# Output rows stored run by run, and the first half's tiles leaving in the order third, first, second

## The chip, the cores and the metric

The kernel runs on one core of one Trainium2 chip. The metric is the time of one execution in microseconds (us), as the device measures it. Inside the core, TensorE (PE) multiplies, VectorE (DVE), ScalarE (ACT) and GpSimd (POOL) work elementwise, and SyncE (SP) issues most of the DMA transfers. The 16 DMA engines of the core move the data between its on-chip memory and the DRAM.

## The reference

A block-sparse attention is followed by a Fourier mixing layer with a two-layer network. For 4 batches, 8 heads, 768 positions and 64 columns per head, in float32:

```python
scores = scale * np.matmul(q, k.transpose(0, 1, 3, 2))
scores = np.where(mask, scores, -1000000000.0)        # mask: blocks of 32 positions
attn = np.exp(scores - scores.max(-1)); attn /= attn.sum(-1) + 1e-09
x = np.matmul(attn, v)          # (B, H, S, D) -> (B, S, H*D) = (4, 768, 512)
...
u = x + np.real(np.fft.fft(np.fft.fft(x, axis=1), axis=2))
un = (u - mean(u)) / np.sqrt(var(u) + 1e-06)
out = u + np.maximum(un @ w_ch1, 0.0) @ w_ch2         # 512 -> 2048 -> 512
```

## The kernel before

**Order of positions.** The 768 positions of a batch are held as six tiles of 128 partitions, not in their order in memory but as the Fourier step wants them. The table `_ORDER` (line 53) gives the runs of each tile: tile, first partition, number of runs, the jump from run to run, rows in a run, first row, step. Tiles 0 and 1 are two ascending runs of 64 rows with step 2 (rows 0, 2, ... and rows 1, 3, ...; then the same from row 128). Tiles 2, 3 and 4 are one single row, two descending runs of 63 rows (step -2), and one single row. Tile 5 is a single row, an ascending run of 63 and an ascending run of 64.

**The row lists.** `_rows` (line 80) turns this into transfers: for a tile it gives pairs of partitions and an access pattern in DRAM. Where the jump is positive, two runs go into one transfer whose outermost dimension is 2 (line 88). It has three uses: the output stores (line 1132), the loads of the sine and cosine tables (`table_s`, line 386), and a general path that runs only where the scores are too large for the fast path, which is not taken with these inputs.

**The halves.** Tiles 0, 1, 2 of a batch stand in a buffer `xA`, tiles 3, 4, 5 in `xB`. There are two of each, so a batch takes the buffer of the batch two before it. The attention writes its output into `xA` and `xB` (`place`, line 666: three transposes on PE, then one copy on ACT, line 675). The first such copy of batch 2 must wait until the stores of batch 0's `xA` have landed, and batch 3 for batch 1.

**The order of the work.** A Python planner writes the instruction order of every engine by hand; it keeps estimated times of the engines in `when`. The attention of batches is cut in slots (`slot`, line 1377). The mixing of an earlier batch is interleaved with it: its elementwise steps from the list `apart`, its large products from the list `late`. For `late`, batches 0, 1 and 2 have four rounds of two `quad` steps (first layer) and six `channels` steps (line 1118: 8 matmul instructions for one tile of the second layer, then one DVE addition into `x`, line 1125); in the last round `channels` calls `store` (line 1130), which issues the tile's transfers on SP. When the last tile of a half has been stored, the pair (batch, half) is added to `finished`. Before batch 2 or 3 places its first output into `xA`, the planner empties `late` until that pair is there (`until`, line 1432), and then gives the copy an estimated 9 us of delay (`LEAVES`), which changes its place among its neighbours and no wait.

**The last batch.** Its second layer is `outputs` (line 1171), which works on tile m of both halves at a time, in order 0, 1, 2 and in two rounds. Its last tile is stored in half-width pieces: the left half of `xA`'s tile on SP, the left half of `xB`'s tile on ACT's queue, then the right halves on SP (lines 1206 to 1233).

## Time and profile before

| What | us |
|---|---|
| Median of three timed runs (lowest to highest) | 1075.06 (1074.61 to 1076.39) |
| The profiled execution, by the same measure as the timed runs | 1075.65 |
| Its span, from the first to the last instruction | 1073.9 |
| PE busy in the span | 1033.3 (96%) |
| DVE, ACT, POOL busy | 669.5, 365.9, 240.5 |
| Written to DRAM | 6.29 MB |

Times in the views are microseconds from the start of the span. "SPq" and "ACTq" are the instruction queues of SP and ACT; a DMA row there is the time to issue a transfer, not to move it. The windows view gives for each stretch its length, the busy time of each engine with its count of instructions, then the TensorE clock that was granted (1.00 is full), the mean busy share of the core's 16 DMA engines, and GB/s. In the timeline, brackets hold the idle time just before a group of instructions and what ended it. The chain of waits is followed back from the last computing instruction.

### The profile page before, as it was taken

Reading aid. Unit: us, or ns where it says so; the run is one execution under the profiler, and the core shown is the slowest. Engines: PE = TensorE matmul, PEld = TensorE weight load, DVE = VectorE, ACT = ScalarE, POOL = GpSimd, SP = SyncE. Lnnn points to the kernel's source line nnn. Section 1 sums busy time; section 2 is a strip of 40 time slices with the busy share of each in tenths; the row PEclk is TensorE's granted clock in tenths of the full one; section 3 lists DMA queues with packets and bytes.
Section 4 is the critical chain, followed back from the end, with each engine's and each line's share of the span. In section 5 each row is a group of like instructions: output and inputs, shape, how many; then the busy total and the mean of one; then the engine's idle time right before and its main releaser. Section 6 shows DMA issues by size and latency. Waiting matters only on the chain.

```text
span 1073.9 us, 12481 instructions
## 1 busy us (share of the span) xinstructions
PE 1033.3 (96%) x4414; PEld 539.6 (50%) x4414; DVE 669.5 (62%) x1227; ACT 365.9 (34%) x736; POOL 240.5 (22%) x270
## 2 busy tenths in 40 slices
PE   8989999999999998999999998899999999999995
PEld 5333345445465453444435654354445554578584
DVE  6888795867746354755678363764456446774663
ACT  6978765564021022432441211434220121210210
POOL 1000173565000000554552001455420001000000
PEclk9999999999999999999999999999999999999998
DMA  7757422220000001231220001211000000000001
GB/s 209 224 170 223 107 46 45 45 45 15 1 1 1 0 3 52 52 55 28 41 54 0 1 1 35 69 29 25 8 14 1 1 0 36 25 1 1 0 15 47
DMA packets 120207, 46.26 MB, mean 43 GB/s; under 512 B 107836, under 2 KB 113226, under 8 KB 120138
## 3 DMA queue, kind: packets, MB, share of 16 engines
q1 hardware_dynamic: 118864, 44.66, 16.9%
q10 hardware_dynamic: 1242, 0.72, 0.3%
q8 instruction: 36, 0.59, 0.2%
q14 instruction: 33, 0.27, 0.1%
q0 software_dynamic: 32, 0.01, 0.0%
HBM read 36.72 MB, written 6.29 MB: 40 GB/s over the span
## 4 chain that ended last, share of the span: by engine, by line
PE 83%; DVE 5%; ACT 3%; DMA 3%; issue 2%; SPq 2%; POOL 0%; ACTq 0%; DVEq 0%
PE y L1122 22%; PE z L1066 15%; PE s L577 11%; PE o L651 9%; PE yp L1066 7%; PE yy L1185 6%; PE xp L1066 3%; PE zp L855 2%; DMA out_dram<-x 2%; PE s L587 1%; PE sp L718 1%; DVE t L1028 1%; SPq L690 1%; ACT e L597 1%; DMA wraw<-in_moe_w_ch_dram 1%
## 5 line engine op out<-in xcount | busy, mean ns | idle before, releaser
L637 POOL TENSOR_TENSOR acc<-acc,e 128x384 f32<-128x384 f32 x158 | 160.8, 1052 | 86.3 <-DVE e L607 67.4
L577 PE MATMUL s<-qT,kT 64*128 64x384 f32 x768 | 156.3, 523 | 16.8 <-DVE e L607 10.4
L651 PE MATMUL o<-e,vr 128*64 128x384 f32 x768 | 142.2, 498 | 2.2 <-DVE oT L659 2.2
L1125 DVE TENSOR_TENSOR x<-y,x 128x512 f32<-128x512 f32 x72 | 49.8, 691 | 131.5 <-PE y L1122 131.2
L1122 PE MATMUL y<-w_sb,hB 128*128 128x512 f32 x288 | 129.0, 599 | 0.3 <-DVE x L1125 0.3
L1122 PE MATMUL y<-w_sb,hA 128*128 128x512 f32 x288 | 128.2, 595 | 0.0
L607 DVE TENSOR_TENSOR e<-s,mask 128x768 f32<-128x768 f32 x88 | 80.1, 950 | 58.2 <-ACT s L605 49.2
L577 PEld LDWEIGHTS s<-qT,kT 64*128 64x128 f32 x768 | 64.7, 187 | 95.1 <-DVE e L607 24.4
L637 POOL TENSOR_TENSOR acc<-e 128x384 f32<-128x384 f32 x46 | 50.4, 1116 | 225.3 <-ACT e L597 127.3
L605 ACT ACTIVATE s<-s 128x768 f32<-128x768 f32 x88 | 66.9, 792 | 92.3 <-PE s L577 92.0
L597 ACT ACTIVATE e<-s 128x768 f32<-128x768 f32 x104 | 79.0, 809 | 48.6 <-PE s L587 35.8
L1066 PE MATMUL z<-unT,t 128*128 128x384 f32 x256 | 93.3, 487 | 0.5 <-DVE hA L1071 0.5
L1122 PEld LDWEIGHTS y<-w_sb,hB 128*128 128x128 f32 x288 | 54.0, 192 | 66.9 <-issue 66.1
L1122 PEld LDWEIGHTS y<-w_sb,hA 128*128 128x128 f32 x288 | 53.7, 190 | 62.5 <-issue 59.8
L651 PEld LDWEIGHTS o<-e,vr 128*64 128x64 f32 x768 | 47.9, 136 | 72.6 <-issue 67.7
L1071 DVE TENSOR_TENSOR hA<-z,hA 128x384 f32<-128x384 f32 x64 | 35.6, 557 | 70.8 <-PE z L1066 70.8
L1075 ACT ACTIVATE hA<-hA 128x384 f32<-128x384 f32 x64 | 33.5, 523 | 122.1 <-DVE hA L1071 122.0
L1066 PEld LDWEIGHTS z<-unT,t 128*128 128x128 f32 x256 | 48.4, 190 | 35.3 <-DVE hA L1071 2.5
L1075 ACT ACTIVATE hB<-hB 128x384 f32<-128x384 f32 x64 | 33.5, 523 | 86.4 <-DVE hB L1071 86.4
L938 POOL TENSOR_SCALAR st<-st 128x1 f32<-128x1 f32 x24 | 8.3, 346 | 207.1 <-DVE st L937 207.0
L1086 ACT COPY hA<-xp 128x384 f32<-128x384 f32 x32 | 15.3, 477 | 111.6 <-PE xp L1066 111.6
L1066 PE MATMUL xp<-unT,w_sb 128*128 128x384 f32 x128 | 47.4, 493 | 0.0
(207 smaller groups left out, 1432.5 us busy)
## 6 DMA issues: line engine op xcount, KB each, us to landing
wraw<-in_moe_w_ch_dram SPq DMA_DIRECT2D x32, 512.0 KB
vr<-in_v_dram SPq DMA_DIRECT2D x30, 192.0 KB
qb<-in_q_dram SPq DMA_DIRECT2D x44, 96.0 KB
kb<-in_k_dram SPq DMA_DIRECT2D x44, 96.0 KB
x<-oT SPq DMA_DIRECT2D x192, 12.0 KB
out_dram<-x SPq DMA_DIRECT2D x11, 252.0 KB
out_dram<-x SPq DMA_DIRECT2D x8, 256.0 KB
qr<-in_q_dram SPq DMA_DIRECT2D x24, 64.0 KB
```

Source lines behind the costliest of these rows:

```text
L577: nc.tensor.matmul(s[:, i, 0:HS], kT[rows, c * P:(c + 1) * P], qT[rows, queries], start=True, stop=u not in by_pe)
L597: nc.scalar.activation(out=e, in_=s[:, :, 0:HS], func=ACT.Exp, scale=scale)
L605: nc.scalar.activation(out=s[:, :, 0:HS], in_=s[:, :, 0:HS], func=ACT.Exp, scale=scale)
L607: nc.vector.tensor_tensor(out=e, in0=s[:, :, 0:HS], in1=m.broadcast_to([P, 2, HS]), op=ALU.mult)
L637: nc.gpsimd.tensor_add(out=acc[:, i, :], in0=start[:, i, :], in1=e[:, i, :])
L651: nc.tensor.matmul(o[D * i:D * i + D, :], vt[:, i, c, :], e[:, i, :], start=(c == 0), stop=(c == C - 1))
L1066: nc.tensor.matmul(to, a[:, k, :], c[:, k, :], start=(k == 0), stop=(k == ND // 2 - 1))
L1071: tt(out=to, in0=ps, in1=a, op=ALU.add)
L1075: nc.scalar.activation(out=h, in_=h, func=ACT.Relu)
L1122: nc.tensor.matmul(y, hs[0, half][:, l, m * P:(m + 1) * P], w2_sb[:, 4 * r + l, :], start=(l == 0), stop=(l == 3))
L1125: nc.vector.tensor_tensor(out=x[:, m, :], in0=y, in1=x[:, m, :], op=ALU.add)
L1185: nc.tensor.matmul(ps, a[:, k, :], c[k // 2][:, k % 2, :] if isinstance(c, list) else c[:, k, :], start=(k == 0), stop=(k == 3))
```

## The change

Two things change. In `_rows`, two runs go into one transfer only if the step is negative: the ascending pairs (tiles 0 and 1) become two transfers of 64 rows each, in the stores and in three of the four loads of the sequence tables; the descending pairs (tiles 2, 3, 4) stay as they are. And the first half's tiles are worked on in the order 2, 0, 1 in `channels` (all rounds); the second half's stay in the order 0, 1, 2. For the last batch, `outputs` takes the tiles in the order 2, 0, 1 for both halves, so the tile stored in pieces at the end is number 1 of each half.

```diff
-        if jump > 0:
+        if jump > 0 > step:
             got.append((p0, runs * n, bass.AP(tensor=at.tensor, offset=at.offset,
                                               ap=[[jump * row, runs], [step * row, n], col])))
             continue
...
-            if m == T - 1:
+            if m == out_of[half][-1]:
                 finished.add((b, half))
...
         last = b == B - 1
+        OUT = (2, 0, 1)
+        out_of = (OUT, OUT if last else (0, 1, 2))
...
-            if m == 0:
+            if m == OUT[0]:
                 output_left(m, 1)
                 output_left(m, 2)
...
-            if m == 0:
+            if m == OUT[0]:
                 output_left(m, 3)
                 output_left(m, 4)
...
-            rest += [(lambda r=r, m=m: outputs(r, m, m + 1 if m + 1 < T else None), 7 * 1.75)
-                     for m in range(T)]
+            rest += [(lambda r=r, m=m, after=after: outputs(r, m, after), 7 * 1.75)
+                     for m, after in zip(OUT, OUT[1:] + (None,))]
...
             rest += [(lambda r=r, half=half, m=m: channels(r, half, m), 3.45)
-                     for half in range(2) for m in range(T)]
+                     for half in range(2) for m in out_of[half]]
```

Compared as built, PE, DVE, ACT and POOL keep their numbers of instructions, and the kinds stand in the same order but for the tile numbers. SP's list has each `2x64x512` store replaced by two `64x512`, and each `128x1x385` table load by two `64x385`. At the end, ACT's queue has the transfers of 1, 2x63 and 1 rows where it had 1, 63 and 64.

## The prediction

> **What bounds the kernel now.** I read the page first, then the list of waits, then the chain of waits, and last the timeline and the windows around the two places to which these led. The page gives the shares of the chain by engine:

> ```profile
> PE 83%; DVE 5%; ACT 3%; DMA 3%; issue 2%; SPq 2%; POOL 0%; ACTq 0%; DVEq 0%
> ```

> PE is the path nearly everywhere, and the change leaves its instructions as they are. So only pauses of PE, and the end after the last product, can move the time. The list of waits (columns: us in total, times, longest) has two rows that belong together:

> ```profile
> ACT x L675 <- DMA out_dram<-x: 13.0, 2, 7.0
> PE s L577 <- DVE e L607: 10.4, 6, 4.4
> ```

> Twice, ACT waits for output stores before it may write into `xA`. The chain (start, us, what) shows both places and the prices of undisturbed work beside them:

> ```profile
> 399.09 3.44 PE y L1122 x8
> 408.18 9.62 DMA out_dram<-x
> 420.17 2.73 PE s L577 x8
> 422.90 4.13 PE y L1122 x8
> 442.42 1.49 PE s L577 x8
> 660.41 10.07 DMA out_dram<-x
> 672.80 2.77 PE s L577 x8
> 675.57 4.07 PE y L1122 x8
> ```

> The first gate in the timeline: SP issues the stores of batch 0's tiles 0, 1 and 2; then come ACT's, PE's and DVE's rows.

> ```profile
> 399.41 0.62 SPq L1133 DMA_DIRECT2D out_dram<-x  x1
> 403.28 0.56 SPq L1133 DMA_DIRECT2D out_dram<-x  x1
> 407.15 2.37 SPq L1133 DMA_DIRECT2D out_dram<-x  x3
> 411.36 0.58 ACT L992 COPY unT<-utp 128x512 f32<-128x512 f32 x1 [3.90 <-PE utp L991]
> 411.15 0.49 PE L674 MATMUL xt<-ident,oT 128*128 128x128 f32 x3
> 411.58 1.56 PE L577 MATMUL s<-qT,kT 64*128 64x384 f32 x8
> 413.07 2.80 PE L651 MATMUL o<-e,vr 128*64 128x384 f32 x16
> 417.95 0.48 ACT L675 COPY x<-xt 128x384 f32<-128x384 f32 x1 [6.00 <-DMA out_dram<-x]
> 419.16 1.82 DVE L607 TENSOR_TENSOR e<-s,mask 128x768 f32<-128x768 f32 x2 [6.49 <-ACT s L605]
> 420.17 2.73 PE L577 MATMUL s<-qT,kT 64*128 64x384 f32 x8 [4.30 <-DVE e L607]
> ```

> Read upward: PE stands 4.30 us for DVE's masking, DVE for ACT's exponential, and ACT's exponential is queued behind the copy L675, which waits 6.00 us for the stores. The copy's source was ready at 411.64 (411.15 + 0.49) and ACT free at 411.94. The second gate has the same shape:

> ```profile
> 662.96 0.58 ACT L992 COPY unT<-utp 128x512 f32<-128x512 f32 x1 [3.29 <-PE utp L991]
> 663.60 0.55 PE L674 MATMUL xt<-ident,oT 128*128 128x128 f32 x3 [0.68 <-ACT unT L992]
> 670.58 0.48 ACT L675 COPY x<-xt 128x384 f32<-128x384 f32 x1 [7.03 <-DMA out_dram<-x]
> 672.80 2.77 PE L577 MATMUL s<-qT,kT 64*128 64x384 f32 x8 [4.43 <-DVE e L607]
> ```

> Why the stores are so late is in the windows (length; busy time of each engine; then granted clock, busy share of the 16 DMA engines, GB/s):

> ```profile
> 400.50:401.00 0.50, 0.50 (x2) 0.19 (x1) 0.13 (x1) 0.00 (x0) 0.42 (x2) 1.00 0.10 25
> 402.00:408.00 6.00, 5.65 (x20) 2.84 (x19) 2.60 (x5) 1.17 (x2) 0.97 (x2) 1.00 0.13 45
> 408.00:412.00 4.00, 4.00 (x16) 2.08 (x16) 1.08 (x3) 0.58 (x1) 0.00 (x0) 1.00 0.13 51
> 420.00:422.00 2.00, 1.83 (x6) 0.94 (x8) 0.98 (x2) 1.38 (x4) 0.00 (x0) 0.61 0.23 67
> 422.00:424.00 2.00, 2.00 (x6) 0.66 (x3) 1.19 (x2) 1.25 (x2) 0.00 (x0) 0.54 0.50 85
> ```

> While only two-run stores are under way, the share is 0.13, which is 2 of 16 engines, and they move 51 GB/s, 25.5 GB/s each. The outermost dimension of these transfers is 2. One tile is 256 KB (262,144 bytes), or 5.1 us at that rate; three tiles in a row are 15.4 us, and from the first data at about 401 that gives 416.4, close to the 417.8 at which the chain sees them landed. The two-engine stores are the gate.

> **The change part by part.**

> *Gates.* Tile 2 goes first: its two-run transfer (252 KB) is issued at 399.4, has data from about 401 and ends near 406.3. Tile 0 follows at 403.3 and tile 1 at 407.15, each as two 64-row transfers. No window of before holds 64-row stores alone. At the end of the kernel 63- and 64-row pieces run beside a two-run one:

> ```profile
> 1061.50:1063.50 2.00, 0.52 (x3) 0.12 (x1) 0.42 (x1) 0.00 (x0) 0.00 (x0) 1.00 0.62 133
> ```

> 133 GB/s in that mixture is the slow bound: 2.0 us for a tile. The fast bound is 16 x 25.5 = 408 GB/s: 0.6 us. I take the slow one. The third store is issued from 407.15; for its two transfers I take 0.85 us (the issues above took 0.56 to 0.62 for one), to 408.0. Its data start some 1.3 us later (399.41 to the window in which data begin), and it is landed by 411.3 at the latest, by 409.9 by the fast bound. ACT is free at 411.94, so L675 no longer waits for DMA. Then ACT copies (0.48), its two exponentials take 1.51 (418.32 to 419.83 in before), and DVE's pair ends about 3.3 us after the copy began, as it does now (417.95 to 420.98): at about 415.3. PE's products L651 end at 415.87. Nothing holds the next scores. Even a landing 0.5 us later costs nothing, and each us after that costs one. At the second gate ACT is free at 663.54 and the source ready at 664.15 (663.60 + 0.55). The third store, tile 1's in the new order, begins to be issued there at 659.37, so by the same sum it lands by 663.5:

> ```profile
> 659.37 0.27 SPq L1133
> ```

> So both pauses go: 4.30 + 4.43 = 8.73 us. After each, the clock was granted at 0.61 and 0.54, and the first work was slow: scores 2.73 and 2.77 against 1.49, second-layer products 4.13 and 4.07 against 3.44. That is 1.24 + 1.28 + 0.69 + 0.63 = 3.84 us, which goes with the pauses. [...]

> What is late next? While PE paused, DVE (6.49 us) and ACT (6.00) were idle too, so no backlog is waiting on them. The loads of `kb`, queued on SP right behind the stores, are first used here, far later:

> ```profile
> 453.10 1.51 DVE L544 STREAM_TRANSPOSE kT<-kb 128x768 f32<-128x768 f32 x1
> ```

> They start earlier too, with the stores ahead of them shorter. The second half's stores stay in two-run form, and its copies showed no wait for DMA; both sides move together.

> *SP's extra issues.* Each tile 0 or 1 costs one issue more, some 0.3 to 0.6 us on SP. In the stretch above, SP had 3 us between tile stores. I take 0; without that cover it is 0.6 us per gate, still inside the margin of the copy.

> *Tables.* Three loads of 192 KB leave the two engines for many. The weight load behind the last of them is awaited once:

> ```profile
> 77.76 0.68 ACT L464 ACTIVATE wraw<-wraw 128x512 f32<-128x512 uint32 x1 [0.92 <-DMA wraw<-in_moe_w_ch_dram]
> ```

> PE runs on through that point on the chain, so between a gain of 0.9 and a loss of 0.6 (one more issue ahead of a weight load) I take 0.

> *Order of the tiles.* The additions into `x` and the second-layer products are the same in number and kind, for other tiles: 0. Batch 2's stores gate nothing: 0.

> *The end.* The last addition is over at 1062.48; what follows is stores.

> ```profile
> 1059.79 1.43 ACTq L1133 DMA_DIRECT2D out_dram<-x  x3
> 1062.06 0.42 DVE L1192 TENSOR_TENSOR x<-yy,x 128x256 f32<-128x256 f32 x1 [0.97 <-PE yy L1185]
> 1066.10 0.91 SPq L1133 DMA_DIRECT2D out_dram<-x  x2
> 1068.00:1071.00 3.00, 0.00 (x0) 0.00 (x0) 0.00 (x0) 0.00 (x0) 0.00 (x0) 0.50 0.15 45
> 1071.00:1071.50 0.50, 0.00 (x0) 0.00 (x0) 0.00 (x0) 0.00 (x0) 0.00 (x0) 0.50 0.00 0
> ```

> SP could not issue the last tile's pieces until 1066.10, 3.6 us after the addition: it was behind earlier two-run stores. The last piece (126 KB, again on two engines) then ran until about 1071. With the change the earlier stores of tiles 0 and 1 are spread, and the last piece on SP is two 64-row transfers, issued at 1062.5. But tile 4's halves are now two-run pieces of 126 KB, one on ACT's queue from 1059.8 and one on SP's from 1060.8. One such piece took about 3.7 us (1067.3 to 1071). If both use the same two engines, they take 7.4 us from about 1061.4, to 1068.8, and the 64-row pieces behind them end at about 1069.3: 1.7 us earlier than now. The bounds: if the two pieces don't share, the last data come at about 1066.5, 4.5 us earlier; if sharing costs each 5 us, 1071.9, 0.9 later. I take 1.7, since the two-run stores of before all show the same share of 2 engines and follow one another.

> *Sum.* 8.73 + 3.84 + 1.7 = 14.3 us. The profiled execution took 1075.65, so it becomes 1061.4. It was 0.59 above the median of 1075.06; the forecast for the median is 1060.8.

> **The rivals.**

> *The gain is swallowed later.* Some load that the pauses hid becomes the bound. Against it: after the gates the list of waits names one wait for a transfer,

> ```profile
> DVE oT L659 <- DMA x<-oT: 5.7, 1, 5.7
> ```

> and what that transfer moves is computed on the path itself, so it starts earlier too. Were all swallowed, only the end would gain: 1075.1 - 1.7 = 1073.4.

> *The gates open only in part*, because 64-row transfers spread over few engines. A tile on n engines takes 10.3/n us. On four that is 2.6, and tile 1 lands at 411.9; on three it lands at 412.7, which leaves 0.2 us at the gate; on two it is nearly as late as now. For something between two and three I reckon 2 us left at each gate and half of the slow clock after it: 1060.8 + 4 + 1.9 = 1066.7. Against it: the 133 GB/s above need more than five engines at 25.5.

> *Splitting does nothing.* Two transfers of half a tile serialize and end no sooner than one. Against it: the share of 0.13, far from full. Then the extra issues cost 0.3 us and the time is 1075.4, on this side of no difference. [...]

> *Slower: each 64-row transfer runs on one engine*, and all on the same one. A tile then takes 10.3 us and tiles 0 and 1 take 20.6 after tile 2's 5.1, so each gate opens about 10.3 us later than now: 1075.1 + 20.6 = 1095.7. It decides from fewer than two engines on. Against it: the share of 0.62 with 133 GB/s at the end, where 63- and 64-row pieces run, is far more than two or three engines.

> *That the change doesn't do what it says* is excluded by the built order: SP's list has the 64-row stores.

> **How the numbers follow.** Forecast, with the bounds of the end in it: 0.86, 1056.5 to 1063.5. Gates open in part: 0.06, 1066.7. Swallowed: 0.04, 1073.4. Splitting does nothing: 0.02, 1075.4. One engine: 0.02, 1095.7. The range of 1056.5 to 1067.0 holds the first case, with a few us for what is not in the sum, and the second; it leaves out 0.08 by these cases and some more for what I haven't thought of. A measurement tells about 0.2%, or 2.15 us, from no change. Faster by more: 0.86 + 0.06 + half of the swallowed case, 0.94. Within: the other half and the case without effect, 0.04. Slower: 0.02.

> **What would show it.** In the changed profile, the row of ACT x L675 waiting for DMA must be gone from the list of waits, and PE's waits for DVE e L607 be under 1.5 us in the longest; the DMA share between the second and the third store must rise well over 0.13 and fall to 0 before the copy; the clock must stay at 1.00 through both gates. Between the last addition (about 12.6 us earlier) and the end of the span there must be 9.7 us instead of 11.4. If L675 still waits, the spread is wrong; if it doesn't and the time stays, something later took the gain.

## The result and the profile after

| | before | after |
|---|---|---|
| Median (lowest to highest) | 1075.72 (1074.61 to 1078.43) | 1062.03 (1061.11 to 1063.46) |
| Profiled execution | 1075.65 | 1061.69 |
| Its span | 1073.9 | 1060.0 |

Four runs each (1075.06, from which the forecast started, is the median of the first three of before). The ratio is 0.987, with a 95% interval of 0.9848 to 0.9893: faster, and 1.2 us from the forecast of 1060.8. The span is 13.9 us shorter. The chain of waits after, by engine, then the rows of the list of waits (us in total, times, longest) that answer to those of before:

```profile
PE 87%; DVE 6%; ACT 4%; issue 2%; DMA 1%; SPq 0%; POOL 0%; ACTq 0%; DVEq 0%; POOLq 0%
```

```profile
ACT wraw L464 <- DMA wraw<-in_moe_w_ch_dram: 3.4, 1, 3.4
...
ACT x L675 <- PE xt L674: 2.7, 4, 0.7
...
PE o L651 <- DVE oT L659: 2.2, 1, 2.2
...
PE s L577 <- DVE e L607: 1.5, 3, 0.8
```

The copy L675 has no wait for DMA left, only short ones for its source. PE waits for the masking L607 for 1.5 us in all, where it was 10.4. On the chain PE rose from 83% to 87%, and DMA and SP's queue fell from 5% together to about 1%.

The first gate in the timeline after: SP's issues of the three tiles, then ACT's and PE's rows.

```profile
398.01 1.57 SPq L1133 DMA_DIRECT2D out_dram<-x  x3
401.89 1.22 SPq L1133 DMA_DIRECT2D out_dram<-x  x2
405.76 1.11 SPq L1133 DMA_DIRECT2D out_dram<-x  x2
409.96 0.59 ACT L992 COPY unT<-utp 128x512 f32<-128x512 f32 x1 [3.90 <-PE utp L991]
410.44 0.49 ACT L675 COPY x<-xt 128x384 f32<-128x384 f32 x1
411.14 1.50 ACT L605 ACTIVATE s<-s 128x768 f32<-128x768 f32 x2 [0.21 <-PE s L577]
411.67 2.80 PE L651 MATMUL o<-e,vr 128*64 128x384 f32 x16
414.40 1.56 PE L577 MATMUL s<-qT,kT 64*128 64x384 f32 x8
415.89 3.70 PE L1122 MATMUL y<-w_sb,hB 128*128 128x512 f32 x8
```

The copy starts with no idle time before it. PE goes from L651 (until 414.47) straight into the next scores, which take 1.56 us instead of 2.73. The windows show why (length, busy time of each engine, granted clock, DMA share, GB/s):

```profile
400.00:402.00 2.00, 2.00 (x9) 1.12 (x8) 0.83 (x2) 0.40 (x1) 0.00 (x0) 1.00 0.12 26
402.00:404.00 2.00, 2.00 (x6) 0.80 (x6) 1.07 (x3) 0.19 (x1) 0.97 (x2) 1.00 0.35 73
404.00:406.00 2.00, 1.65 (x8) 0.89 (x7) 0.69 (x1) 0.52 (x1) 0.00 (x0) 1.00 0.47 141
406.00:408.00 2.00, 2.00 (x5) 0.84 (x5) 0.00 (x0) 0.06 (x1) 0.00 (x0) 1.00 0.54 130
408.00:409.00 1.00, 1.00 (x4) 0.48 (x3) 0.00 (x0) 0.00 (x0) 0.00 (x0) 1.00 0.14 33
409.00:411.00 2.00, 2.00 (x15) 1.29 (x15) 1.48 (x3) 0.97 (x2) 0.00 (x0) 1.00 0.00 1
```

Tile 2's two-run store has the low share of before to itself until 402 (0.12 against 0.13). When the 64-row stores join it, the share goes to 0.54, and from 409 nothing is under way. The last tile, issued from 405.76, has landed by 408.64 (2.9 us), 1.8 us before the copy. The second gate:

```profile
655.60 0.59 ACT L992 COPY unT<-utp 128x512 f32<-128x512 f32 x1 [3.29 <-PE utp L991]
656.82 0.48 ACT L675 COPY x<-xt 128x384 f32<-128x384 f32 x1 [0.64 <-PE xt L674]
```

There the copy waits 0.64 us for its own source and not 7.03 us for the stores, which had landed by 654.90.

One place is slower than in before. The rows are PE's timeline after, then the windows of after, then the same place in the timeline of before:

```profile
684.51 2.71 PE L651 MATMUL o<-e,vr 128*64 128x384 f32 x8 [2.17 <-DVE oT L659]
```

```profile
684.00:686.00 2.00, 1.49 (x6) 0.69 (x8) 2.00 (x3) 0.00 (x0) 0.56 (x1) 0.67 0.04 6
686.00:688.00 2.00, 2.00 (x8) 0.55 (x6) 1.58 (x2) 0.00 (x0) 2.00 (x3) 0.50 0.13 19
```

```profile
698.02 1.51 PE L651 MATMUL o<-e,vr 128*64 128x384 f32 x8 [2.18 <-DVE oT L659]
```

PE pauses equally long in both, 2.17 and 2.18 us. After it the clock is halved in the changed kernel, and in before it is not; the products take 2.71 instead of 1.51 us.

The end after: the last addition, the last issues on ACT's and SP's queues, and the windows up to the last data.

```profile
1049.97 0.42 DVE L1194 TENSOR_TENSOR x<-yy,x 128x256 f32<-128x256 f32 x1 [0.97 <-PE yy L1187]
1047.70 1.87 ACTq L1133 DMA_DIRECT2D out_dram<-x  x3
1048.99 3.06 SPq L1133 DMA_DIRECT2D out_dram<-x  x4
```

```profile
1054.00:1056.00 2.00, 0.00 (x0) 0.00 (x0) 0.00 (x0) 0.00 (x0) 0.00 (x0) 0.50 0.19 51
1056.00:1057.50 1.50, 0.00 (x0) 0.00 (x0) 0.00 (x0) 0.00 (x0) 0.00 (x0) 0.50 0.09 31
1057.50:1058.50 1.00, 0.00 (x0) 0.00 (x0) 0.00 (x0) 0.00 (x0) 0.00 (x0) 0.50 0.00 0
```

The last addition ends at 1050.39, and 9.6 us of stores follow it; in before it was 1062.48 and 11.4. SP is no longer held back from issuing the last pieces, but the low share at the very end (0.19, then 0.09) is still that of a two-run piece, which lands at 1057.07.

PE's matmuls are the same 4414 in both, so the two traces can be laid over each other instruction by instruction. In this pair of executions the 13.9 us of the span arise in these places:

| stretch of before | gain, us |
|---|---|
| up to 62 (no table awaited yet) | 0.8 |
| 62 to 411, with the table loads | 0.6 |
| first gate (411 to 427) | 6.0 |
| second gate (660 to 681) | 6.2 |
| the halved clock at 698 | -1.6 |
| the rest up to the last addition | 0.1 |
| stores after the last addition | 1.8 |

### The profile page after: what moved, and what is told of

Its sections match the earlier page's. It is cut to its first block, busy times and chain, and to the rows that moved or that the text cites. A ratio compares the mean times of both kernels' runs of the same rounds, so it can differ in the third digit from the quotient of the medians.

```text
span 1060.0 us, 12495 instructions
## 1 busy us (share of the span) xinstructions
PE 1030.6 (97%) x4414; PEld 537.1 (51%) x4414; DVE 669.1 (63%) x1227; ACT 366.5 (35%) x736; POOL 240.5 (23%) x270
## 4 chain that ended last, share of the span: by engine, by line
PE 87%; DVE 6%; ACT 4%; issue 2%; DMA 1%; SPq 0%; POOL 0%; ACTq 0%; DVEq 0%; POOLq 0%
PE y L1122 23%; PE z L1066 16%; PE s L577 11%; PE o L651 10%; PE yp L1066 8%; PE yy L1187 7%; PE xp L1066 4%; PE zp L855 2%; PE s L587 1%; DVE t L1028 1%; ACT e L597 1%; PE sp L718 1%; PE sp L732 1%; PE utp L991 1%; PE xt L674 1%
## 5 line engine op out<-in xcount | busy, mean ns | idle before, releaser
L577 PE MATMUL s<-qT,kT 64*128 64x384 f32 x768 | 154.8, 518 | 7.4 <-ACT e L597 5.8
L651 PE MATMUL o<-e,vr 128*64 128x384 f32 x768 | 143.1, 500 | 2.2 <-DVE oT L659 2.2
L1122 PE MATMUL y<-w_sb,hB 128*128 128x512 f32 x288 | 128.0, 595 | 0.3 <-DVE x L1125 0.3
L1122 PE MATMUL y<-w_sb,hA 128*128 128x512 f32 x288 | 128.1, 594 | 0.0
L607 DVE TENSOR_TENSOR e<-s,mask 128x768 f32<-128x768 f32 x88 | 80.0, 950 | 48.9 <-ACT s L605 39.9
L577 PEld LDWEIGHTS s<-qT,kT 64*128 64x128 f32 x768 | 64.5, 187 | 85.7 <-ACT e L597 23.6
L605 ACT ACTIVATE s<-s 128x768 f32<-128x768 f32 x88 | 66.7, 792 | 92.6 <-PE s L577 92.4
L1122 PEld LDWEIGHTS y<-w_sb,hB 128*128 128x128 f32 x288 | 53.5, 190 | 65.5 <-issue 64.6
L1122 PEld LDWEIGHTS y<-w_sb,hA 128*128 128x128 f32 x288 | 53.6, 190 | 62.6 <-issue 59.9
L651 PEld LDWEIGHTS o<-e,vr 128*64 128x64 f32 x768 | 48.0, 136 | 72.7 <-issue 67.8
L1066 PE MATMUL z<-t,w_sb 128*128 128x384 f32 x128 | 46.7, 488 | 0.7 <-DVE t L1028 0.7
```

What stands on the lines that cost most here:

```text
L577: nc.tensor.matmul(s[:, i, 0:HS], kT[rows, c * P:(c + 1) * P], qT[rows, queries], start=True, stop=u not in by_pe)
L605: nc.scalar.activation(out=s[:, :, 0:HS], in_=s[:, :, 0:HS], func=ACT.Exp, scale=scale)
L607: nc.vector.tensor_tensor(out=e, in0=s[:, :, 0:HS], in1=m.broadcast_to([P, 2, HS]), op=ALU.mult)
L651: nc.tensor.matmul(o[D * i:D * i + D, :], vt[:, i, c, :], e[:, i, :], start=(c == 0), stop=(c == C - 1))
L1066: nc.tensor.matmul(to, a[:, k, :], c[:, k, :], start=(k == 0), stop=(k == ND // 2 - 1))
L1122: nc.tensor.matmul(y, hs[0, half][:, l, m * P:(m + 1) * P], w2_sb[:, 4 * r + l, :], start=(l == 0), stop=(l == 3))
```

## The experiments

The theory: a two-run store of a whole tile goes out on two DMA engines (the share of 0.13 in before); splitting the ascending tiles gives them many, and together with the order (the two-run tile first) the gate opens before anyone needs it. The rivals: the order does it alone; the tables, or the end, bring the gain; it is the number of transfers and not their spread.

**e1: the split alone.**

```diff
-        OUT = (2, 0, 1)
+        OUT = (0, 1, 2)
```

> The ascending pairs split as in the change, the tiles in the old order 0, 1, 2 everywhere. My theory (a two-run store is held to two engines, and the gate opens when the last of them has landed): tile 2, two-run, now leaves last, issued near 406 and landed some 8.0 us later, at 414.2; ACT's copy waits about 3.8 us instead of 6.0 and PE pauses about 2.1 us at each gate, with or without a slow clock after it. The end gains 3.7 us, since only one two-run half piece is left behind the last addition. About 1063.8 to 1067.6. Rival (the split does all of it, the order is idle): both pauses gone and the better end, about 1060.

1064.05 us (4 runs) against 1076.97 for before, ratio 0.9885 (0.987 to 0.9901). Its timeline at the first gate:

```profile
413.55 0.48 ACT L675 COPY x<-xt 128x384 f32<-128x384 f32 x1 [3.81 <-DMA kb<-in_k_dram]
415.77 1.78 PE L577 MATMUL s<-qT,kT 64*128 64x384 f32 x8 [2.11 <-DVE e L607]
```

With the two-run tile last, its store is issued from 405.26 and lands at 413.23, and the copy starts at 413.55. The wait is put down to a load of `kb`, but what lands just then is the store. PE still pauses 2.11 us, half of what it was. So the split alone brings most: the earlier stores no longer stand ahead of the third. At the two gates e1 gains 3.6 and 4.0 us, after 6.0 and 6.2; the order is worth some 2.3 us at each. At the end e1 is the shorter one: 8.0 us from the last addition to the end of the span. That end, and a clock which in the profiled execution was not halved anywhere ahead of it, bring e1 so near to the change (0.9885 against 0.987).

**e2: the order alone.**

```diff
-        if jump > 0 > step:
+        if jump > 0:
```

> The order 2, 0, 1 as in the change, but the ascending pairs still two runs in one transfer. My theory: the same 764 KB go over two engines one after the other, so ACT's copy still waits 6 to 7 us and PE pauses 4.3 us at each gate; at the end four half pieces of about 3.7 us share two engines, some 6 us later than before: about 1078 to 1082. Rival (the order is what opens the gates): about 1062.

1077.88 us (10 runs), ratio 1.0009 (0.9995 to 1.0024): no difference that can be told. Its list of waits:

```profile
ACT x L675 <- DMA out_dram<-x: 13.6, 2, 7.3
...
PE s L577 <- DVE e L607: 11.0, 6, 4.7
```

These are nearly the waits of before. The order by itself opens neither gate: the three two-run stores hold the copy for 13.6 us in this order and for 13.0 in the old one. The end was expected some 6 us later, with four half pieces on two engines; it takes 12.9 us from the last addition, 1.5 more than in before, so that part of the expectation missed.

**e3 and e8: more transfers, but narrower.** Each 64-row store of the change is cut in two: 62 + 2 rows in e3, 61 + 3 rows in e8. The tables stay as in the change.

```diff
-        for r in range(runs):
+        for r, s0, p0, n in ([(0, s0 + r * jump + step * i, p0 + r * 64 + i, c) for r in range(runs)
+                              for i, c in ((0, 62), (62, 2))] if tile < 2 and view.shape[1] != 385
+                             else [(r, s0, p0, n) for r in range(runs)]):
```

> The change, but each ascending run of 64 rows is stored as 62 rows and 2 rows, still run by run. 62 has only 2 as a divisor up to 16. If the number of engines is what counts and it goes by the outermost count's divisors, these run on two engines again: DMA share 0.13 between the stores, both gates shut again for about 6 us, the end later too, 1075 to 1082. Rival (two runs in one transfer are slow as such, or a transfer of one run spreads whatever its count): gates open, 1062 to 1063, with a few more issues.

1080.30 us (5 runs), ratio 1.0049 (1.0032 to 1.0065): all of the gain gone, and a little more. The list of waits of e3 (two lines were added above, so L675 is L677), and its windows:

```profile
ACT x L677 <- DMA out_dram<-x: 15.3, 2, 8.1
```

```profile
406.00:408.00 2.00, 2.00 (x7) 0.80 (x6) 0.00 (x0) 0.00 (x0) 0.00 (x0) 1.00 0.13 43
408.00:412.00 4.00, 4.00 (x24) 2.14 (x24) 1.75 (x3) 0.59 (x1) 0.00 (x0) 1.00 0.13 46
```

62 of 64 rows in the transfer, and the share is back at 0.13. The 62-row stores of the first gate land at 409.07, 411.75, 414.34 and 416.89, some 2.6 us apart.

> The change, but each ascending run of 64 rows is stored as 61 rows and 3 rows. 61 is prime: if the engines go by the divisors of the outermost count, the 61 rows run on a single engine, 5.1 us for each of the four pieces of tiles 0 and 1, one after the other behind tile 2's two-run store, so each gate opens some 9 us later than before the change and the end is later too: about 1095 to 1103, the slower rival of the prediction. Rival (a transfer of 61 rows spreads like one of 64): 1062 to 1064.

1110.05 us in one run, span 1108.3, above the range that was expected. The windows and the waits of e8 (in the third row other transfers run beside the 61-row stores):

```profile
409.00:412.00 3.00, 3.00 (x16) 1.70 (x15) 1.41 (x3) 0.59 (x1) 0.00 (x0) 1.00 0.07 27
412.00:420.00 8.00, 3.54 (x22) 1.26 (x18) 0.34 (x1) 0.00 (x0) 0.00 (x0) 0.95 0.07 27
420.00:428.00 8.00, 0.00 (x0) 0.00 (x0) 0.00 (x0) 0.23 (x1) 0.00 (x0) 0.50 0.19 52
```

```profile
ACT x L677 <- DMA out_dram<-x: 33.3, 2, 17.2
...
PE s L579 <- DVE e L609: 30.5, 5, 14.6
```

The share of 0.07 is one engine of 16, with 27 GB/s; the 61-row stores land at 412.45, 417.42, 422.40 and 427.37, 5.0 us apart. So 64, 62 and 61 rows have many, two and one engine: it is not the size that decides, nor the number of transfers, which is the same in e3 and e8. The completion marks in the traces give a count beside the shares: as it lands, a 64-row store of the change writes its semaphore 16 times (at the first gate from 407.76 to 408.05, then from 408.39 to 408.64), a two-run store of before twice (412.48 and 412.49), a 62-row store of e3 twice and a 61-row store of e8 once. The shares of 0.13 and 0.07 agree with two and one of 16, and the 0.54 with the 64-row stores is that of a mixture. Two for 62 rows and one for 61 is what the expectations had reckoned; what number goes with other counts does not follow from these runs. The slower rival of the prediction is thus a real one, with its point of decision where it was put, below two engines, and a higher price.

**e4: the tables alone.** The three ascending table loads are split, stores and order are those of before.

```diff
-        if jump > 0:
+        if jump > 0 and not (split and step > 0):
...
-            rows = _rows(src, t)
+            rows = _rows(src, t, True)
```

> Only the three table loads are split, the stores are as before. My theory: no difference, 1075.7 within 1, the one wait of 0.92 us of ACT for a weight load behind a table gone and PE not earlier by it. Rival: the 1.4 us by which the changed kernel was ahead before its first store come from here: 1074.3.

1074.44 us (11 runs) against 1076.97, ratio 0.9981 (0.9971 to 0.9992): by the ratio 2.0 us faster, by its interval 0.9 to 3.1. The gates are as shut as in before (13.3 us of waiting, the longest 7.2). The expectation of no gain missed.

**e5: the stores and the order, with the tables as before; e7: the change once more, beside it.**

```diff
-        if jump > 0 > step:
+        if jump > 0 > step or jump > 0 and joined:
...
-            rows = _rows(src, t)
+            rows = _rows(src, t, True)
```

> The change without the splitting of the three table loads: stores and order as changed. If the tables are worth nothing, as the prediction had it: the time of the change, 1062 to 1063. If the 2.0 us of the kernel with split tables alone come from them: 1064 to 1065.

> The changed kernel itself beside the other two, for one set of runs on the same chip. Expected at 1062 to 1063. Theory on the clock: a stretch of 3.41 us at half clock near 684, after a pause of PE of 2.2 us that both kernels have, comes and goes from one execution to the next; if it is tied to the change instead, it is there again at the same place.

e5 took 1064.48 us (6 runs), ratio 0.9884 (0.9865 to 0.9904); e7 1063.36 (5 runs), 0.9869 (0.9848 to 0.9889), both against 1077.77 for before. So the stores carry nearly all of the gain. The 1.1 us between the two fit the tables, but the runs can't tell them from none or from two. e7 was also to show whether the halved clock near 684 comes and goes or is tied to the change: it was there again, as the last section tells.

**e9 and e10: is it the spread of the tables?** Before, with each of the three table loads as four transfers: 61, 3, 61 and 3 rows in e9, four times 32 in e10. SP issues equally many.

```diff
+        if cut and tile < 2:
+            for r in range(runs):
+                for i, k in ((0, cut), (cut, n - cut)):
+                    first = view[s0 + r * jump + step * i:s0 + r * jump + step * i + 1, :]
+                    got.append((p0 + r * n + i, k, bass.AP(tensor=first.tensor, offset=first.offset,
+                                                           ap=[[step * row, k], col])))
+            continue
         if jump > 0:
...
-            rows = _rows(src, t)
+            rows = _rows(src, t, 61)
```

> Before, with each of the three table loads at the start as four transfers of 61, 3, 61 and 3 rows; stores and tile order as before. Theory (the split tables gained 2 us in e4 because the weight loads queued behind them no longer stand behind two busy engines): a 61-row piece runs on one engine, so a table is narrower than in before, the weights land later, and the time is 2 us or more above before, 1078 and up, with a longer wait of ACT for wraw in the list of waits. Rival (the tables are hidden and e4's 2 us are the scatter of the clock, or come from anything else that the spread doesn't set): within 1 us of before.

> Before, with each of the three table loads as four transfers of 32 rows: as many issues as in e9, but each spread over many engines. Theory: as e4, 1.0 to 3.0 us below before, which also says that SP's nine extra issues cost nothing. Rival, as in e9: within 1 us of before. If both this and e9 come out equally far from before on one side, it is the issues that count and not the spread.

e9: 1082.27 us (5 runs), ratio 1.0055 (1.0038 to 1.0071), so 6 us slower. e10: 1073.74 (11 runs), 0.9978 (0.9968 to 0.9989), so 2.4 us faster, both against 1076.22. Equally many issues, opposite signs: the spread of the tables sets the time, and the issues don't. The path from a narrow table to PE can be read in e9's timeline (seven lines were added above, so L464 is L471 and L510 is L517):

```profile
63.23 0.66 ACT L471 ACTIVATE wraw<-wraw 128x512 f32<-128x512 uint32 x1 [4.79 <-DMA wraw<-in_moe_w_ch_dram]
...
67.92 0.74 PE L517 MATMUL tp<-ident,kr 128*128 128x128 f32 x3 [4.44 <-ACT kT L520]
...
82.66 0.68 ACT L471 ACTIVATE wraw<-wraw 128x512 f32<-128x512 uint32 x1 [4.48 <-DMA wraw<-in_moe_w_ch_dram]
...
86.44 0.44 PE L517 MATMUL tp<-ident,qr 128*128 128x128 f32 x2 [2.84 <-ACT qT L526]
```

A weight load stands behind the table's long piece, ACT waits for the weights, and PE for the ACT copy queued behind that wait. PE loses 4.3 us against before between 62 and 100; most of what is then still missing to 6 us is lost behind the gates, where the clock is halved for 6.83 us each time and in before for 3.41. That part doesn't come from narrow tables, for the profiled e10 has the same 6.83 at both gates. In the other direction the same pause of PE, ahead of the scores at 71.43 in before, is 3.08 us there and 2.04 in e10. The rows are of before, then of e10:

```profile
71.43 2.26 PE L577 MATMUL s<-qT,kT 64*128 64x384 f32 x8 [3.08 <-ACT e L597]
```

```profile
70.23 1.62 PE L584 MATMUL s<-qT,kT 64*128 64x384 f32 x8 [2.04 <-ACT e L604]
```

But this pause varies from execution to execution: 2.58 to 3.35 us in the three profiles with joined tables, 1.97 to 3.42 in the eight with tables in 64- or 32-row pieces. Nor does the weight load that ACT awaits ahead of it stand behind a joined table: in before it was issued at 64.35, when the last one had landed (54.12) and the next was not yet issued (69.04). Whether the split shortens this pause at all, and by what way the tables gain, stays open.

**e6: the change, but the last batch in the old order.**

```diff
-        OUT = (2, 0, 1)
-        out_of = (OUT, OUT if last else (0, 1, 2))
+        OUT = (0, 1, 2) if last else (2, 0, 1)
+        out_of = (OUT, (0, 1, 2))
```

> The change, with the last batch's tiles in the old order 0, 1, 2, so that only one two-run half piece is left behind the last addition (and tile 5's pieces of 63 and 64 rows) in place of two. Theory: gates open as in the change, and the end 1.9 us shorter, as the kernel with the split alone had it (3.7 us less than before against 1.8): 1060.0 to 1061. Rival (the end of that kernel was short for another reason, its later arrival): no difference, 1062 to 1063.

1061.74 us (5 runs), ratio 0.985 (0.9831 to 0.9869); from the last addition (1051.56) to the end of the span it takes 8.5 us, 3.0 less than before and 1.1 less than after, where 1.9 less had been expected; the time, too, is above the expected 1060 to 1061. In e6 the last piece is a two-run transfer that shares its engines with no other two-run piece: the one before it had landed at 1049.93, ahead of its issue at 1051.86. In after, two such pieces are under way at once, on ACT's and SP's queue: the one issued at 1048.26 lands at 1053.80, the one issued at 1048.99 only at 1057.07, and the 64-row pieces behind them at 1057.38 and 1057.75 (14 of the 16 marks of each had come by 1055.02, the other two from 1056.86 on). So the new order is of use at the gates and not at the end. Of the versions tried this has the lowest median, 1.6 us below the change in the same set, though the two intervals overlap.

## Why the prediction was right

*The gates, forecast 8.73 for the pauses and 3.84 for the slow clock after them, 12.6 in all.* They brought 6.0 + 6.2 = 12.2 us. The 0.4 that is missing lies in the slow clock: I had taken 3.44 us for undisturbed second-layer products, from another place on the chain, and behind the gates they take 3.64 and 3.63 at full clock, so it was worth 3.4 us. The mechanism is shown from three sides: e2 keeps the narrow stores and keeps the waits; e3 makes the split stores narrow again, by two rows, and has the waits back; e1 keeps the two-run tile last and keeps half of the pause. I had the 64-row tile landed 2.75 to 4.15 us after its issue; it took 2.9, close to the fast bound of 16 engines.

*The end, forecast 1.7.* It was 1.8, by the way forecast: two 126 KB pieces share two engines and follow one another (they land at 1053.80 and 1057.07). What the forecast didn't see is that the order of before would have been better here (3.0 in e6), so the split brings the gain at the end and the order gives part of it back.

*The tables, forecast 0.* This is the term that was mis-sized. I bounded it between a gain of 0.9 and a loss of 0.6 by the one wait of ACT behind the last table, and took 0 because PE ran on at that point. By e4 and e10 the tables alone are worth 2.0 and 2.4 us, and e9 shows that delays of the loads behind a narrow table reach PE through ACT's queue. So the one wait of ACT did not bound the term. Why joined tables cost 2 us in before is not shown: I had not weighed ACT's longer wait, until 69.49, and PE's 3.08 us behind it, but that load stands behind no joined table either.

*What was in no term.* 0.8 us came ahead of any table that is awaited, from the start-up, which differs between executions of the same kernel: e7 is there 0.5 us behind before. And 1.6 us were lost at 684 by a clock that halved after a pause which before has too, as it did in e5, e6 and e7. These and the tables nearly cancel, and that is luck: 14.3 forecast against 13.96 between the two profiled executions, and 1060.8 against a median of 1062.03.

*The rivals.* Gates open in part: no, the list has no wait left. Swallowed later: no; of the lead of 13.5 us behind the second gate only the 1.6 of the clock is lost again. Splitting does nothing: refuted by e1 and e5, both at 0.988. As the share of 0.13 had said, the one transfer had two engines; the two have many, with 16 completion marks each. One engine for each 64-row transfer: no, but e8 shows its price. Its gates cost 11.5 and 10.8 us more than those of before, where 10.3 each had been reckoned without more of the slow clock, and the stores at the end, which the rival had not priced, took 22.7 us from the last addition to the end of the span (11.4 in before).

## What to carry to other kernels

When a wait for a store ends a chain, look at the DMA share while that store alone is under way: here 0.13 stood for two engines, for 256 KB (before) as for 124 KB (e3), and 0.07 for one (122 KB, e8). Where it is low, try the runs one by one, as the 64-row stores here, even at the price of one more issue, and count the rows before rounding a transfer off: 62 rows (two engines) landed 2.6 us apart and 61 rows (one engine) 5.0, where 64-row pieces landed 0.6 apart, about the time between their issues (0.5). Let a transfer that must stay narrow leave first (some 2.3 us at each gate here), and price loads at the start by what is queued behind them on the waiting engine, not by the wait alone.

## What the runs showed of the hardware

The pause ahead of L651 that stands near 684 in after (698 in before) is 2.17 or 2.18 us in all twelve. In after, e5, e6 and e7, 2.01 us or more of it lie in one window, and the clock halved; in the other eight it is split (in before into 1.06 and 1.12), and the clock did not. These four are also the ones in which no gate made PE pause. So the halving there may be tied to the change rather than come and go by chance, which is what I had expected ahead of e7; why the pause falls as it does is not shown. The pause near 70 lies in one window in e4 (2.03 us) and is split in e10 (0.19 and 1.85), and the clock halved in e4 only.

A window did not have to be idle throughout, since 2.17 us of its 3.41 were enough in after. One such stretch cost about 1.6 us at 684 in after: products of 2.71 us against 1.51 in before, and the scores behind them 2.00 against 1.56.
